# Query transposes of six batches moved from PE to DVE, with loads by groups of 32 features

## Chip, cores and metric

One core of one Trainium2 chip. The metric is the device time of one execution in microseconds. Short names: PE is the matmul engine, DVE the vector engine, ACT the scalar engine, POOL is GpSimd, SP the engine whose queue issues nearly all transfers. The granted clock is the clock that PE was allowed, as a share of its full speed; the mean of a run was 0.976 to 0.993 in the runs told here.

## The reference

```python
# q, k, v: (8 batches, 8 heads, 576 rows, 64 features), fp32
kv  = np.einsum('bhsd,bhse->bhde', k, v)
out = np.einsum('bhsd,bhde->bhse', q, kv)
rms = np.sqrt(np.mean(out * out, axis=-1, keepdims=True) + 1e-06)
x   = (out / rms * g_norm)              # reordered to (4608 tokens, 512)
h   = x @ w_in                          # 512 -> 2048
y   = np.maximum(h, 0.0) ** 2 @ w_out   # 2048 -> 512
```

## The kernel before

It works in nine strips of 512 tokens. Each strip has an "up" part (x @ w_in, relu squared) and a "down" part (@ w_out). In strips 1 to 8 both are made of seven products by a Strassen scheme, and in strip 0 the down part alone is. Between the products it puts the attention of later strips in slices. The product with kv takes a query with its features on the partitions, so each pair of heads is transposed there, against the identity, and copied out of PSUM by ACT:

```python
    def load(b, p, q_eng):              # a pair of heads: k, v, q
        ...
        whole = src[b, hs, 0 : C * P].rearrange("h (sp c) d -> sp h c d", c=C)
        ...                             # q and k, one transfer a head, pieces of 256 bytes
        t = qkv_pool.tile([P, C, 2, D], FP32, name=n, tag=n)
        for h in range(2):
            eng.dma_start(out=t[:, :, h, :], in_=whole[:, h])

    def transposed_query(b, p):
        t = main.pop(("q", b, p))
        ps = apsum.tile([P, C, P], FP32, name="t_ps", tag="at")
        for c in range(C):              # C = 4
            nc.tensor.transpose(ps[:, c, :], flat(t[:, c]), ident)
        qT[b, p] = qt_pool.tile([P, C, P], FP32, name="qT", tag="qT")
        nc.scalar.copy(qT[b, p], ps)
        if b % 2:                       # the last 64 rows of two batches, as one tile
            ...                         # one more transpose (tr_ps) and copy (qT_rest)

    def out_rows(n):                    # which rows of the output a tile of 128 tokens is
        ...
        return [(slice(0, P), out[b * S : b * S + C * P, :].rearrange("(sp c) e -> c sp e", c=C)[c_b])]

    def stream():                       # the next block of w_out, 1 MB, three buffers
        ...
            nc.sync.dma_start(out=w_blk[u], in_=w_out[B_OUT[u[1]]])

    def down(s, p, i):                  # product p of the down part, half i
        ...
        product(p, i, lambda fc: a[:, fc, ts(i, P)], lambda fc: w[:, fc, :], FQ)
        if i == 0: return
        ...
        stream()                        # asks for a block when a product is done
        ...                             # store: copy to o_sb, then SP issues out_rows
```

Products of one part run in the order 1, 2, 6, 5, 7, 3, 4. Each has one of the PSUM banks A (two buffers), B and C.

Of the kernel before, what the change touches and what calls it, by code (L numbers as in the profile page):

```python
# [9 lines left out]
FP32 = mybir.dt.float32  # L10
# [9 lines left out]
def kernel(  # L20
# [26 lines left out]



    nc = tc.nc  # L50
    P = 128
    B, H, S, D = q.shape
# [3 lines left out]
    NP = H // 2  # L56
    FC = d_ff // P
    C = S // P
# [5 lines left out]
    STRIP = NT * P  # L64
    TH = STRIP // 2
    N_STRIP = N_TILE // NT
    EPS = 1e-6
    const = ctx.enter_context(tc.tile_pool(name="const", bufs=1))
    wpool = ctx.enter_context(tc.tile_pool(name="wpool", bufs=1))
    qkv_pool = ctx.enter_context(tc.tile_pool(name="qkv", bufs=3))  # L70
    rest_pool = ctx.enter_context(tc.tile_pool(name="rest", bufs=1))
    qt_pool = ctx.enter_context(tc.tile_pool(name="qt", bufs=NP + 1))
# [18 lines left out]
    def load(b, p, q_eng):  # L91
        hs = slice(2 * p, 2 * p + 2)
        for n, src, eng in (("k", k, nc.sync), ("v", v, nc.sync), ("q", q, q_eng)):
            whole = src[b, hs, 0 : C * P].rearrange("h (sp c) d -> sp h c d", c=C)
            if n == "v":
                t = qkv_pool.tile([P, 2, C, D], FP32, name=n, tag=n)
                eng.dma_start(out=t, in_=whole)  # L97
            else:
# [4 lines that stand above are left out]
            main[n, b, p] = t  # L103
# [4 lines left out]
    v_rest = const.tile([P, 2, H, D], FP32, name="v_rest")  # L108
    q_rest = {}

    def load_rest(b, eng):
        h = b % 2
        half = slice(REST * h, REST * (h + 1))
        if h == 0:
            q_rest[b // 2] = rest_pool.tile([P, H, D], FP32, name="q_rest", tag="q_rest")
        for t, src in ((k_rest[half], k), (v_rest[half, h], v), (q_rest[b // 2][half], q)):
            eng.dma_start(out=t, in_=src[b, :, C * P : S].rearrange("h s d -> s h d"))

    units = [(b, p) for b in range(B) for p in range(NP)]
    to_load = iter(units)  # L120
# [1 line left out]
    def load_next(q_eng=nc.sync):  # L122
        u = next(to_load, None)
        if u is not None:
            load(*u, q_eng)
# [105 lines left out]
    def convert(n):  # L231
        while converted[0] < min(n, len(conversions)):
            fn, a = conversions[converted[0]]
            fn(a)
            converted[0] += 1

    nc.gpsimd.memset(k_rest, 0.0)
    nc.gpsimd.memset(v_rest, 0.0)
    load_next(nc.gpsimd)
    load_rest(0, nc.gpsimd)  # L240
    for i in range(2):
        load_next(nc.gpsimd)
# [12 lines left out]
    qT, kvd, x_n, xt = {}, {}, {}, {}  # L255
    flat = lambda t: t.rearrange("p h d -> p (h d)")

    def transposed_query(b, p):
        t = main.pop(("q", b, p))
        ps = apsum.tile([P, C, P], FP32, name="t_ps", tag="at")  # L260
        for c in range(C):
            nc.tensor.transpose(ps[:, c, :], flat(t[:, c]), ident)  # L262
        qT[b, p] = qt_pool.tile([P, C, P], FP32, name="qT", tag="qT")
        nc.scalar.copy(qT[b, p], ps)
        if b % 2:
            t = q_rest[b // 2][:, 2 * p : 2 * p + 2]
            ps = apsum.tile([P, P], FP32, name="tr_ps", tag="at")
            nc.tensor.transpose(ps, flat(t), ident)
            qT["rest", b // 2, p] = qt_pool.tile([P, P], FP32, name="qT_rest", tag="qT_rest")
            nc.scalar.copy(qT["rest", b // 2, p], ps)  # L270

    def key_value(b, p):
        tk, tv = main.pop(("k", b, p)), main.pop(("v", b, p))
        ps = apsum.tile([P, P], FP32, name="kv_ps", tag="at")
        for c in range(C):
            nc.tensor.matmul(ps, lhsT=flat(tk[:, c]), rhs=tv[:, :, c, :], start=(c == 0), stop=False)  # L276
        nc.tensor.matmul(  # L277
            ps, lhsT=flat(k_rest[:, 2 * p : 2 * p + 2]), rhs=v_rest[:, b % 2, 2 * p : 2 * p + 2],
            start=False, stop=True,
        )  # L280

        d = kv_pool.tile([P, P], FP32, name="kvd", tag="kvd")
        nc.gpsimd.memset(d[0:D, D:P], 0.0)
        nc.gpsimd.memset(d[D:P, 0:D], 0.0)
        nc.scalar.copy(d[0:D, 0:D], ps[0:D, 0:D])
        nc.scalar.copy(d[D:P, D:P], ps[D:P, D:P])
        kvd[b, p] = d
        if b < 2:
            if p == 0:
                load_next(nc.sync if b else nc.gpsimd)  # L290
        else:
            load_next()
            if p == NP - 1 and b + 1 < B:
                load_rest(b + 1, nc.sync)

    def query(n):
# [17 lines left out]
        nc.vector.reduce_sum(out=ms, in_=by_head(sq), axis=AX.X)  # L314
        nc.vector.tensor_scalar(out=ms, in0=ms, scalar1=1.0 / D, scalar2=EPS, op0=ALU.mult, op1=ALU.add)
        r = small.tile([P, H], FP32, name="rms", tag="rms")
# [35 lines left out]
    for b in range(B):  # L352
        for p in range(NP):
            slices += [(transposed_query, (b, p)), (key_value, (b, p))]
        first = b // 2 * PAIR + (C if b % 2 else 0)
        ns = list(range(first, first + C + b % 2))
        for i, n in enumerate(ns + [None]):
            if n is not None:
                slices.append((query, (n,)))
            if i > 0:  # L360
                slices.append((features, (ns[i - 1],)))
                if ns[i - 1] % NT == NT - 1:
                    if ns[i - 1] // NT:
                        slices.append((sums_x, (ns[i - 1] // NT,)))
                    ready[ns[i - 1] // NT] = len(slices)
    slice_at = [0]

    def attend(n):
        while slice_at[0] < min(n, len(slices)):
            fn, a = slices[slice_at[0]]  # L370
            fn(*a)
            slice_at[0] += 1

    def out_rows(n):
        m, c = divmod(n, PAIR)
        if c == C:
            return [
                (slice(REST * h, REST * (h + 1)), out[(2 * m + h) * S + C * P : (2 * m + h + 1) * S, :])
                for h in range(2)
            ]  # L380
        b, c_b = (2 * m, c) if c < C else (2 * m + 1, c - C - 1)
        return [(slice(0, P), out[b * S : b * S + C * P, :].rearrange("(sp c) e -> c sp e", c=C)[c_b])]

    ORDER = (1, 2, 6, 5, 7, 3, 4)
    BANK = {1: "A", 6: "A", 7: "A", 4: "A", 5: "B", 3: "B", 2: "C"}
# [85 lines left out]
    w_blk[0, 1], w_blk[0, 2], w_blk[0, 5] = w_first  # L471
    to_stream = iter([(s, p) for s in range(N_STRIP) for p in ORDER if (s, p) not in w_blk])

# [6 lines left out]
    def down(s, p, i):  # L480
        if i == 0:
            open_bank(p)
        a = gq[s, {1: 11, 2: 21, 6: 11, 5: 1, 7: 12, 3: 21, 4: 22}[p]]
        w = w_blk[s, p]
        product(p, i, lambda fc: a[:, fc, ts(i, P)], lambda fc: w[:, fc, :], FQ)
        if i == 0:
            return
        del w_blk[s, p]
        if s > 0 or p not in (1, 2, 5):
            stream()  # L490
        if p == 1:
            minus(nc.vector, gq[s, 11], gq[s, 1], gq[s, 11])
        if p == 2:
            minus(nc.vector, gq[s, 21], gq[s, 21], gq[s, 11])

        def store(th, eh):
            def f(b, a=None):
                o = osb_pool.tile([P, 2, DH], FP32, name="o_sb", tag="o_sb")
                if a is None:
                    nc.scalar.copy(o, b)  # L500
                else:
                    nc.vector.tensor_tensor(out=o, in0=b, in1=a, op=ALU.add)
                for t in range(2):
                    for part, rows in out_rows(NT * s + 2 * th + t):
                        nc.sync.dma_start(out=rows[:, ts(eh, DH)], in_=o[part, t, :])
            return f

        combine(p, store(0, 0), store(0, 1), store(1, 0), store(1, 1))

    for i in range(ready[0]):  # L510
        attend(i + 1)
        convert((i + 1) // 4)
    for s in range(N_STRIP):
        attend(ready[s])
# [76 lines left out]
```

## Time and profile before

| | |
|---|---|
| median of the first three runs | 1031.32 us |
| PE, DVE, ACT busy | 96 %, 41 %, 26 % of the span |
| PE's waits, all of the span | 33.6 us, nearly all before 175 us |
| transposes of queries on PE | 144, in slots of 0.109 us |

The profile comes from one execution. In a row of the timeline, the first column is the start in microseconds from the beginning of the span and the second is how long the merged row lasted; `x4` is the number of instructions, and `[20.13 <-PE ps_A L399]` is how long the engine was idle before and what released it. In a list of waits the numbers are the total wait, how often, and the longest. Line numbers differ between the kernels: L399 of before is L442 of the changed kernel. The lines that carry the bound are shown in the prediction.

### The profile page before, as it was taken

Reading aid. Unit: us, or ns where it says so; the run is one execution under the profiler, and the core shown is the slowest. Engines: PE = TensorE matmul, PEld = TensorE weight load, DVE = VectorE, ACT = ScalarE, POOL = GpSimd, SP = SyncE. Lnnn points to the kernel's source line nnn. Section 1 sums busy time; section 2 is a strip of 40 time slices with the busy share of each in tenths; the row PEclk is TensorE's granted clock in tenths of the full one; section 3 lists DMA queues with packets and bytes.
Section 4 is the critical chain, followed back from the end, with each engine's and each line's share of the span. In section 5 each row is a group of like instructions: output and inputs, shape, how many; then the busy total and the mean of one; then the engine's idle time right before and its main releaser. Section 6 shows DMA issues by size and latency. Waiting matters only on the chain.

```text
span 1029.7 us, 12226 instructions
## 1 busy us (share of the span) xinstructions
PE 992.0 (96%) x4864; PEld 852.2 (83%) x4864; DVE 423.9 (41%) x769; ACT 264.0 (26%) x546; POOL 19.5 (2%) x83
## 2 busy tenths in 40 slices
PE   3599999999999999999999999999999999999998
PEld 3444688888888888888888888888888888888887
DVE  2777974344233533333333325332632334413420
ACT  3568620321033112221132113210321122102200
POOL 4000000000000000000000000000000000000000
PEclk9699999999999999999999999999999999999999
DMA  9389797134422433244413640274012420251032
GB/s 222 121 235 276 240 326 226 47 81 135 156 82 62 138 133 102 62 114 145 145 32 85 187 163 1 62 207 165 33 31 95 159 74 1 92 175 61 1 133 71
DMA packets 119081, 125.58 MB, mean 122 GB/s; under 512 B 78224, under 2 KB 102800, under 8 KB 111344
## 3 DMA queue, kind: packets, MB, share of 16 engines
q1 hardware_dynamic: 118336, 123.36, 39.2%
q0 software_dynamic: 528, 1.44, 0.6%
q8 instruction: 38, 0.62, 0.2%
q14 instruction: 19, 0.16, 0.0%
q10 hardware_dynamic: 160, 0.00, 0.0%
HBM read 108.00 MB, written 16.78 MB: 121 GB/s over the span
## 4 chain that ended last, share of the span: by engine, by line
PE 87%; DVE 4%; DMA 4%; ACT 3%; SPq 1%; issue 1%; DVEq 0%; ACTq 0%
PE ps_A L399 45%; PE ps_B L399 23%; PE ps_C L399 11%; PE x_ps L309 3%; DMA raw<-in_moe_w_in_dram 2%; PE kv_ps L276 2%; PE xt_ps L336 2%; DMA raw<-in_moe_w_out_dram 2%; PE t_ps L262 1%; ACT w_c L161 1%; DVE wt L195 1%; SPq L97 1%; ACT raw L164 1%; DVE w_c L185 1%; PE kv_ps L277 1%
## 5 line engine op out<-in xcount | busy, mean ns | idle before, releaser
L399 PE MATMUL ps_A<-w_blk,gt 128*128 128x256 f32 x1120 | 249.9, 379 | 0.0
L399 PEld LDWEIGHTS ps_A<-w_blk,gt 128*128 128x128 f32 x1120 | 211.1, 190 | 27.9 <-PE x_ps L304 0.2
L399 PE MATMUL ps_A<-x_t,w_in 128*128 128x256 f32 x768 | 181.6, 379 | 0.6 <-DVE gt L459 0.6
L399 PEld LDWEIGHTS ps_A<-x_t,w_in 128*128 128x128 f32 x768 | 143.8, 190 | 19.5 <-DVE gt L459 1.0
L399 PE MATMUL ps_B<-w_blk,gt 128*128 128x256 f32 x544 | 121.5, 379 | 0.0
L399 PEld LDWEIGHTS ps_B<-w_blk,gt 128*128 128x128 f32 x544 | 102.4, 190 | 13.6 <-issue 0.2
L195 DVE TENSOR_TENSOR gt<-gt 128x512 f32<-128x512 f32 (+1 forms) x54 | 66.2, 1225 | 68.2 <-PE ps_A L399 37.6
L409 ACT COPY snap<-ps_A 128x512 f32<-128x512 f32 x82 | 48.1, 586 | 164.8 <-PE ps_A L399 164.8
L459 DVE TENSOR_TENSOR gt<-ps_C,snap 128x512 f32<-128x512 f32 x32 | 22.1, 692 | 147.8 <-PE ps_C L399 147.8
L460 DVE SCALAR_TENSOR_TENSOR gt<-gt 128x512 f32<-128x512 f32 x96 | 66.4, 692 | 3.3
L459 DVE TENSOR_TENSOR gt<-ps_A,snap 128x512 f32<-128x512 f32 x32 | 22.1, 691 | 108.4 <-PE ps_A L399 108.1
L399 PE MATMUL ps_B<-x_t,w_in 128*128 128x256 f32 x256 | 60.5, 379 | 0.0
L399 PE MATMUL ps_B<-xT,w_in 128*128 128x256 f32 x256 | 60.5, 379 | 0.0
L399 PE MATMUL ps_A<-xT,w_in 128*128 128x256 f32 x256 | 60.5, 379 | 0.0
L399 PE MATMUL ps_C<-xT,w_in 128*128 128x256 f32 x256 | 60.5, 379 | 0.0
L399 PE MATMUL ps_C<-w_blk,gt 128*128 128x256 f32 x256 | 57.7, 380 | 0.0
L314 DVE TENSOR_REDUCE ms<-sq 128x8 f32<-128x512 f32 x36 | 24.6, 684 | 76.9 <-ACT sq L312 76.9
L399 PEld LDWEIGHTS ps_C<-xT,w_in 128*128 128x128 f32 x256 | 48.6, 190 | 6.6
L399 PEld LDWEIGHTS ps_A<-xT,w_in 128*128 128x128 f32 x256 | 48.2, 190 | 6.3
L399 PEld LDWEIGHTS ps_C<-w_blk,gt 128*128 128x128 f32 x256 | 47.7, 190 | 6.2 <-issue 0.2
L399 PEld LDWEIGHTS ps_B<-x_t,w_in 128*128 128x128 f32 x256 | 47.6, 190 | 5.9
L399 PEld LDWEIGHTS ps_B<-xT,w_in 128*128 128x128 f32 x256 | 47.6, 190 | 5.9
(83 smaller groups left out, 867.7 us busy)
## 6 DMA issues: line engine op xcount, KB each, us to landing
w_blk<-w_out SPq DMA_DIRECT2D x60, 1024.0 KB, 5.2
k<-in_k_dram SPq DMA_DIRECT2D x64, 128.0 KB, 3.3
v<-in_v_dram SPq DMA_DIRECT2D x32, 256.0 KB, 3.6
raw<-in_moe_w_in_dram SPq DMA_DIRECT2D x16, 512.0 KB, 5.1
raw<-in_moe_w_out_dram SPq DMA_DIRECT2D x16, 512.0 KB, 5.4
out_dram<-o_sb SPq DMA_DIRECT2D x64, 128.0 KB, 5.0
q<-in_q_dram SPq DMA_DIRECT2D x56, 128.0 KB, 3.4
w_out<-wt SPq DMA_DIRECT2D x8, 512.0 KB, 4.5
```

What stands on the lines that cost most here:

```text
L97: eng.dma_start(out=t, in_=whole)
L161: nc.scalar.activation(c, high_f, AF.Abs)
L164: nc.scalar.activation(r, low, AF.Copy, scale=2.0**-29)
L195: eng.tensor_tensor(out=out, in0=a, in1=b, op=ALU.subtract)
L276: nc.tensor.matmul(ps, lhsT=flat(tk[:, c]), rhs=tv[:, :, c, :], start=(c == 0), stop=False)
L309: nc.tensor.matmul(o, lhsT=qT[b, p][:, c_b, :], rhs=kvd[b, p], start=True, stop=True)
L314: nc.vector.reduce_sum(out=ms, in_=by_head(sq), axis=AX.X)
L336: nc.tensor.transpose(ps[:, p, :], t[:, ts(p, P)], ident)
L399: nc.tensor.matmul(bank[BANK[p]][:, i, :], lhsT=lhsT(k), rhs=rhs(k), start=p in (1, 5, 2) and i == 0 and k == 0, stop=k == n - 1, skip_gro ...
L409: nc.scalar.copy(snap[p], b)
L459: nc.vector.tensor_tensor(out=o, in0=b, in1=a, op=ALU.add)
L460: nc.vector.scalar_tensor_tensor(out=o, in0=o, scalar=0.0, in1=o, op0=ALU.max, op1=ALU.mult)
```

## The change

The intent is to relieve PE, the bound. The change transposes on DVE in squares of 32x32 (SQ = 32): the load puts each group of 32 features of a pair of heads on its own 32 partitions, with 16 rows of 32 features behind one another on each; one DVE instruction (STREAM_TRANSPOSE, 128x512) then gives features on partitions and tokens along the row. Its price is that a load has pieces of 128 bytes and comes in four transfers, and that the tokens come in a permuted order, which the stores undo in four pieces of 32 rows. Batches 0 and 1 stay on PE.

```diff
+    SQ = 32
+    Q_ON_PE = 2
...
+            if n == "q" and b >= Q_ON_PE:
+                t = qkv_pool.tile([P, 4 * C, SQ], FP32, name=n, tag=n)
+                for a in range(4):
+                    h, f = divmod(a * SQ, D)
+                    eng.dma_start(
+                        out=t[ts(a, SQ)],
+                        in_=src[b, 2 * p + h, 0 : C * P, f : f + SQ].rearrange("(i k) f -> i k f", k=4 * C),
+                    )
...                                      (load_rest: 8 small transfers in place of one)
     def transposed_query(b, p):
         t = main.pop(("q", b, p))
+        if b >= Q_ON_PE:
+            qT[b, p] = qt_pool.tile([P, C, P], FP32, name="qT", tag="qT")
+            nc.vector.transpose(out=flat(qT[b, p]), in_=flat(t))
+            if b % 2 and p == NP - 1:
+                rest = qt_pool.tile([P, NP, 4, SQ], FP32, name="qT_rest", tag="qT_rest4", bufs=1)
+                nc.vector.transpose(
+                    out=rest, in_=squares(q_rest[b // 2]).rearrange("p k q f -> p q k f")
+                )
...
+            return
...
-        return [(slice(0, P), out[...].rearrange("(sp c) e -> c sp e", c=C)[c_b])]
...                                      (batches 0 and 1 as before)
+        return [
+            (ts(k, SQ), rows.rearrange("(i k) e -> k i e", k=4 * C)[4 * c_b + k]) for k in range(4)
+        ]
```

More of the change, by code (lines that the diff above doesn't have):

```diff
@@ L94, in load @@
             whole = src[b, hs, 0 : C * P].rearrange("h (sp c) d -> sp h c d", c=C)
-            if n == "v":
+            if n == "q" and b >= Q_ON_PE:
[6 more added lines that the diff above has]
+                    )
+            elif n == "v":
                 t = qkv_pool.tile([P, 2, C, D], FP32, name=n, tag=n)
@@ L109 @@
     q_rest = {}
+    squares = lambda t: t.rearrange("p h d -> p (h d)").rearrange("p (k q f) -> p k q f", k=4, f=SQ)
     def load_rest(b, eng):
@@ L116, in load_rest @@
         for t, src in ((k_rest[half], k), (v_rest[half, h], v), (q_rest[b // 2][half], q)):
-            eng.dma_start(out=t, in_=src[b, :, C * P : S].rearrange("h s d -> s h d"))
+            if src is q and b >= Q_ON_PE:
+                t = squares(q_rest[b // 2])
+                for a in range(4):
+                    hq, f = divmod(a * SQ, D)
+                    for kq in range(2):
+                        eng.dma_start(
+                            out=t[ts(a, SQ), 2 * h + kq],
+                            in_=src[b, hq::2, C * P + kq * SQ : C * P + (kq + 1) * SQ, f : f + SQ].rearrange(
+                                "p i f -> i p f"
+                            ),
+                        )
+            else:
+                eng.dma_start(out=t, in_=src[b, :, C * P : S].rearrange("h s d -> s h d"))
     units = [(b, p) for b in range(B) for p in range(NP)]
@@ L259, in transposed_query @@
         t = main.pop(("q", b, p))
+        if b >= Q_ON_PE:
[5 more added lines that the diff above has]
+                    out=rest, in_=squares(q_rest[b // 2]).rearrange("p k q f -> p q k f")
+                )
+                for i in range(NP):
+                    qT["rest", b // 2, i] = rest[:, i].rearrange("p k f -> p (k f)")
+            return
         ps = apsum.tile([P, C, P], FP32, name="t_ps", tag="at")
@@ L381, in out_rows @@
         b, c_b = (2 * m, c) if c < C else (2 * m + 1, c - C - 1)
-        return [(slice(0, P), out[b * S : b * S + C * P, :].rearrange("(sp c) e -> c sp e", c=C)[c_b])]
+        rows = out[b * S : b * S + C * P, :]
+        if b < Q_ON_PE:
+            return [(slice(0, P), rows.rearrange("(sp c) e -> c sp e", c=C)[c_b])]
+        return [
+            (ts(k, SQ), rows.rearrange("(i k) e -> k i e", k=4 * C)[4 * c_b + k]) for k in range(4)
+        ]
     ORDER = (1, 2, 6, 5, 7, 3, 4)
```

## The prediction

> **What bounds the kernel now.** I read first the shares of each engine and the forty slices, then the waits of PE, then the order of PE's work in one strip, and last the end of the program. The page and its chain of waits:
>
> ```profile
> PE 992.0 (96%) x4864; PEld 852.2 (83%) x4864; DVE 423.9 (41%) x769; ACT 264.0 (26%) x546; POOL 19.5 (2%) x83
> ...
> PE   3599999999999999999999999999999999999998
> ...
> PEclk9699999999999999999999999999999999999999
> DMA  9389797134422433244413640274012420251032
> ...
> PE 87%; DVE 4%; DMA 4%; ACT 3%; SPq 1%; issue 1%; DVEq 0%; ACTq 0%
> ```
>
> PE is the bound: 96% busy, and from the third slice on every slice is at 9 or more. DVE (41%) and ACT (26%) have much room, and so have the DMA engines after the first 200 us. The chain that ended last is PE for 87% of the span. A busy PE alone is weak evidence, so I looked for its waits. This is the list of what PE waited for, whole:
>
> ```profile
> PE xt_ps L336 <- DVE x_n L325: 11.5, 4, 5.9
> PE t_ps L262 <- POOL ident masks.py:199: 9.4, 1, 9.4
> PE tr_ps L268 <- ACT qT L264: 3.7, 2, 2.2
> PE t_ps L262 <- DMA q<-in_q_dram: 3.4, 1, 3.4
> PE kv_ps L276 <- ACT qT L264: 2.9, 1, 2.9
> PE kv_ps L276 <- DMA v<-in_v_dram: 1.3, 1, 1.3
> PE ps_A L433 <- ACT xT L337: 0.8, 1, 0.8
> PE ps_A L399 <- DVE gt L459: 0.6, 1, 0.6
> ```
>
> (Columns: who waited for whom, us in all, times, longest.) Together 33.6 us, and the busy time by stretches puts nearly all of it into the first 200 us (PE is busy 69.6 of the first 100, 97.4 of the second, and 100 of 100 in each from 200 to 820). The query transposes of batches 0 and 1, which wait here, stay on PE. The six batches that the change moves run in the part where PE waits for nothing. So an instruction taken off PE there shortens the span by the slot it held, and by no more. That slot is read from the timeline of PE around two of the groups to be removed:
>
> ```profile
> 545.33 0.60 PE L262 MATMUL t_ps<-ident,q 128*128 128x128 f32 x4
> 545.76 0.27 PE L268 MATMUL tr_ps<-ident,q_rest 128*128 128x128 f32 x1
> 545.87 1.89 PE L399 MATMUL ps_A<-x_t,w_in 128*128 128x256 f32 x8
> ...
> 553.90 1.89 PE L399 MATMUL ps_A<-x_t,w_in 128*128 128x256 f32 x8
> 555.62 0.60 PE L262 MATMUL t_ps<-ident,q 128*128 128x128 f32 x4
> ```
>
> The first column is the start, the second the duration. Matmuls overlap: the durations (273 ns for one transpose) are no cost. The cost is from start to start: 545.76 - 545.33 = 0.43 us for four transposes, 545.87 - 545.76 = 0.11 us for the fifth, about 0.109 us each.
>
> [...]
>
> **The change part by part.**
>
> Off PE: 6 batches x 4 pairs x 4 = 96 transposes of whole tiles, and 3 x 4 = 12 of the rests, in all 108 of 144. 108 x 0.109 = **11.8 us off the path**. The order of everything else on PE stays, as the comparison of instruction orders shows.
>
> Off ACT: 24 copies of 586 ns and 12 of 273 ns, 17.3 us. ACT isn't the bound: worth 0.
>
> Onto DVE: 24 transposes into qT and 3 for the rests, each 128x512, [...]. PE waits for DVE where a bank is to be freed: product 4 needs bank A after DVE has read product 7, with one product (1.73 us) between. The order of DVE in the changed kernel has each transpose behind a product's own two operations, never between the product and the read that frees its bank. [...] Worth 0, at worst some tenths a group.
>
> Query loads: two transfers a pair of heads become four, of 128-byte pieces instead of 256. 24 x 1024 = 24,576 packets more, and 3,072 more for the rests (8 transfers of 128 pieces in place of 512 pieces, per batch), on top of 119,081. A load of k, v and q (2,304 packets) took about 3.3 us of all 16 engines around 541 us (sum of the DMA shares of those slices), 23 ns a packet on one engine; so 27,648 packets are some 40 us of the 16 engines' time (estimate), spread over 500 us where they are a third busy. The loads are issued three pairs ahead, some 30 us before use, and the k, v and q of a pair land in 3.3 to 3.6 us. Hidden.
>
> DMA queue of SP: each issue holds it. 24 x 2 more query issues at 0.59 us (28 us), 6 x 7 more for the rests at 0.63 (26 us), and the permuted token order splits each of the 48 half-width output stores of batches 2 to 7 in four: 144 more at about 0.39 (56 us). These 110 us fall where SP now waits: its list of waits has 282.5 us for ps_A and 256.2 us for kv_ps alone. The danger is a late w_out block behind these issues. A block is asked for when a product ends and needed two products later, 2 x 6.91 = 13.8 us; it lands in 5.2 us (10.1 at worst). A store of eight pieces in front of it takes 8 x 0.39 = 3.1 us, a query and rest load in front some 4 to 6 us more than now. Normally that fits; with the worst landing it does not quite.
>
> The end: here the stores are on the path.
>
> ```profile
> 1023.77 1.89 PE L399 MATMUL ps_A<-w_blk,gt 128*128 128x256 f32 x8
> 1023.99 1.27 PEld L399 LDWEIGHTS ps_A<-w_blk,gt 128*128 128x128 f32 x6
> 1025.70 0.59 ACT L500 COPY o_sb<-ps_A 128x512 f32<-128x512 f32 x1 [20.13 <-PE ps_A L399]
> 1026.31 0.81 SPq L505 DMA_DIRECT2D out_dram<-o_sb  x2
> ```
>
> After the last matmul comes one copy, then two issues in 0.81 us, then 2 us to landing. The last strip is of batch 7, so two become eight, one behind the other: 6 x 0.39 = **2.3 us onto the path**; a smaller piece may land a little sooner, so I take 2.2.
>
> Sum: 1031.3 - 11.8 + 2.2 = **1021.7 us**, 0.9% less.
>
> **The rivals.**
> (1) The whole gain and more, past 2%: that needs 20.6 us. 108 transposes at 190 ns would give it, but the starts show 109 ns; and there are no waits of PE behind 200 us to be freed. I see no way to it.
> (2) DVE becomes the wait: it blocks in order on a query transfer or on its own queue, and PE waits for a bank. For it: one wait of PE on DVE of 0.6 us shows that the margin is thin at one place. Against: DVE idles over half of each strip, waiting for products of PE. If each of 27 transposes cost PE 0.3 us, 8 us come back: 1030 us.
> (3) A late block of w_out behind the many issues on SP. For it: the arithmetic above, with some 3 us to spare in bad cases. Against: three buffers, and landings of 5.2 us mostly. Two us in each of the five or six strips with loads: 1032 us.
> (4) Stores cost more than at the end alone, if a 32-row store is issued or lands slower than I take it: another 1 to 3 us at the end.
>
> **Range and chances.** The 11.8 us are firm to within 0.5 and the 2.2 to within 1. The rivals 2 and 3 can only add time, so the range is longer above: 1019.5 to 1026.0, predicted 1021.8. Faster by over 2% (below 1010.7) 0.02; slower by over 2% (above 1051.9) needs a failure of the DMA schedule in every strip, 0.02; within 2% 0.96.
>
> **What would show it right or wrong.** PE has 4864 - 108 = 4756 matmuls, and is still at 100 of 100 us in the stretches from 200 to 820; its list of waits has no new row above 1 us. [...] The time from the last matmul to the end grows by about 2.2 us, with eight issues near 0.39 us in it. The w_blk transfers still land in about 5 us. If PE shows waits for DVE products of L459 or idles in the first down products of a strip, rival 2 or 3 holds. [...]

## The result

The changed kernel took **1022.45 us** (median of four runs, 1021.19 to 1022.73), against 1031.09 us for the kernel before (four runs). The ratio is 0.9915, with a 95 % interval of 0.9897 to 0.9932. A ratio is the mean time of one kernel's runs over that of the other's in the same rounds, so it isn't quite the ratio of the medians. The gain is under 2 %, but the interval leaves 1 well outside.

The page of the changed kernel, its busy row, the slices of PE and the chain:

```profile
PE 979.3 (96%) x4756; PEld 842.2 (83%) x4756; DVE 440.2 (43%) x796; ACT 248.6 (24%) x510; POOL 19.6 (2%) x83
...
PE   3599899999999999999999999999999999999997
...
PE 87%; DMA 4%; DVE 4%; ACT 3%; SPq 1%; issue 1%; DVEq 0%; ACTq 0%
```

108 instructions are gone from PE, and PE is the bound as before. What PE waited for, those rows that begin to matter:

```profile
PE xt_ps L373 <- DVE x_n L362: 14.7, 4, 5.9
...
PE ps_A L442 <- DVE gt L502: 0.6, 1, 0.6
```

There is no new row. After 190 us the last one alone remains, as before. At the place that the prediction showed, the transposes are gone from the timeline of PE:

```profile
537.39 1.89 PE L442 MATMUL ps_C<-xT,w_in 128*128 128x256 f32 x8
539.11 1.89 PE L442 MATMUL ps_A<-x_t,w_in 128*128 128x256 f32 x8
```

539.11 - 537.39 = 1.72 us is the slot of the product alone; in the kernel before 0.43 and 0.11 us of transposes stood between these two. DVE's timeline shows where the work went:

```profile
540.11 0.69 DVE L503 SCALAR_TENSOR_TENSOR gt<-gt 128x512 f32<-128x512 f32 x1
540.72 0.70 DVE L288 STREAM_TRANSPOSE qT<-q 128x512 f32<-128x512 f32 x1
544.56 0.69 DVE L502 TENSOR_TENSOR gt<-ps_A,snap 128x512 f32<-128x512 f32 x1 [3.14 <-PE ps_A L442]
```

Behind the transpose DVE still waits 3.14 us for PE. The end of the program, first the copy, then the row of the last stores from the view of the tile o_sb (durations of one issue: least, median, most; first and last start):

```profile
1014.45 0.59 ACT L543 COPY o_sb<-ps_A 128x512 f32<-128x512 f32 x1 [20.13 <-PE ps_A L442]
```
```profile
L548 SPq DMA_DIRECT2D out_dram<-o_sb x8: 314/419/421, 1015.1 to 1018.2; - x8
```

To account for the 9.0 us between the two profiled spans (1029.7 and 1020.7), I cut each at two marks: the first matmul of strip 1, and ACT's copy behind the last matmul.

| profiled run | to strip 1 | strip 1 to last copy | last copy to end | span |
|---|---|---|---|---|
| before | 175.00 | 850.70 | 4.0 | 1029.7 |
| changed | 175.60 | 838.85 | 6.25 | 1020.7 |
| difference | +0.6 | -11.85 | +2.25 | -9.0 |

The middle stretch turned out to be a very sharp measure: over the runs below it repeats to 0.01 us when nothing in it changes. The first stretch is not: it lies between 173.1 and 175.6 us in ten of the twelve profiles, with no order by kernel, so the 0.6 is noise. Another run of the changed kernel had 173.1.

### The profile page after: what moved, and what is told of

The parts are those of the page before. It is cut to its first block, busy times and chain, and to the rows that moved or that the text cites. A ratio compares the mean times of both kernels' runs of the same rounds, so it can differ in the third digit from the quotient of the medians.

```text
span 1020.7 us, 12318 instructions
## 1 busy us (share of the span) xinstructions
PE 979.3 (96%) x4756; PEld 842.2 (83%) x4756; DVE 440.2 (43%) x796; ACT 248.6 (24%) x510; POOL 19.6 (2%) x83
## 3 DMA queue, kind: packets, MB, share of 16 engines
q1 hardware_dynamic: 149728, 123.38, 40.9%
## 4 chain that ended last, share of the span: by engine, by line
PE 87%; DMA 4%; DVE 4%; ACT 3%; SPq 1%; issue 1%; DVEq 0%; ACTq 0%
PE ps_A L442 45%; PE ps_B L442 23%; PE ps_C L442 12%; PE x_ps L346 3%; DMA raw<-in_moe_w_out_dram 2%; PE kv_ps L313 2%; DMA raw<-in_moe_w_in_dram 2%; PE xt_ps L373 2%; ACT w_c L187 1%; DVE w_c L211 1%; SPq L109 1%; DVE wt L221 1%; ACT raw L190 1%; PE kv_ps L314 1%; SPq L114 0%
```

## The experiments

The theory: the gain is the slots on PE and the loss the longer end; nothing else that the change adds reaches the path. Rivals: the gain came from freed copies or PSUM buffers; DVE's work holds PE up somewhere; or the many issues on SP do. All kernels gave correct results. This table has them all, in the order told below; "median" and "ratio" are of the timed runs, the three stretches of the profiled one.

| run | to strip 1 | strip 1 to copy | to end | median us | ratio to before |
|---|---|---|---|---|---|
| e0 changed kernel again | 173.1 | 838.84 | 6.2 | 1021.20 | 0.9900 |
| e2 PE transposes put back, unread | 173.3 | 850.70 | 6.25 | 1034.16 | 1.0018 |
| e4 before, stores split only | 175.4 | 850.70 | 6.4 | 1034.03 | 1.0020 |
| e1 rows in order, stores whole | 174.7 | 838.85 | 3.7 | 1019.58 | 0.9885 |
| e3 each DVE transpose three times | 173.7 | 838.85 | 6.2 | 1021.55 | 0.9908 |
| e3b each nine times | 175.1 | 880.37 | 6.25 | 1063.84 | 1.0316 |
| e6 loads by 16 features | 177.2 | 853.91 | 6.2 | 1033.78 | 1.0032 |
| e8 loads by 8 rows | 174.1 | 841.08 | 6.2 | 1023.98 | 0.9942 |
| e7 = e1 with loads by 16 | 174.2 | 843.87 | 3.7 | 1023.84 | 0.9936 |
| e5 = e1 with all batches on DVE | 189.4 | 838.84 | 3.8 | 1034.03 | 1.0025 |

**e0: the changed kernel again.** No edit.

> The changed kernel unaltered, for noise and as the measure of the other runs of this call. Mine: 1022.3 us within 1.5; from the start of strip 1 on PE to the last copy 838.9 us within 0.3 (before: 850.7); from the last copy to the end 6.2 us within 0.3 (before: 4.0). If the 0.6 us by which strip 1 began later than before in the first profile belong to the change, they come again; if they are noise of the start, they do not.

838.84 and 6.2 us came again, and the 0.6 us of a later start did not.

**e2: the transposes of PE put back.** Their results go to PSUM and nobody reads them.

```diff
             nc.vector.transpose(out=flat(qT[b, p]), in_=flat(t))
+            ps = apsum.tile([P, C, P], FP32, name="t_ps", tag="at")
+            for c in range(C):
+                nc.tensor.transpose(ps[:, c, :], flat(t)[:, ts(c, P)], ident)
+            if b % 2: ...                # the same for the rest, tr_ps
```

> The changed kernel with the 108 transposes of PE put back where they were, their results unread. Theory (a removed transpose is worth its slot of 0.109 us on PE and nothing else in the change has a cost inside the strips): 11.8 us more than the changed kernel, about 1034 us, 2.3 us above the kernel before, and 850.7 us from strip 1 to the last copy. Rival (the gain came from the copies taken off ACT or the PSUM buffers set free, or PE hides such transposes): clearly less than 11 us comes back.

The stretch is 850.70 us again, to the hundredth that of the kernel before, although ACT makes none of the moved copies and DVE makes the transposes of the six batches as well. So the gain is the slots: 11.85 / 108 = 0.110 us each. The copies taken off ACT were worth nothing. The PSUM buffers came back together with the transposes, so this run alone does not part the two; but 0.110 us is the slot read from the starts, and in the kernel before PE has after 190 us no wait for such a buffer, only the 0.6 us for bank A.

**e4: the stores alone.** The kernel before, whose stores of batches 2 to 7 are cut in four.

```diff
-        return [(slice(0, P), out[b * S : b * S + C * P, :].rearrange("(sp c) e -> c sp e", c=C)[c_b])]
+        rows = out[b * S : b * S + C * P, :].rearrange("(sp c) e -> c sp e", c=C)[c_b]
+        if b < 2:
+            return [(slice(0, P), rows)]
+        return [(ts(k, 32), rows[ts(k, 32)]) for k in range(4)]
```

> The kernel before with only its stores of batches 2 to 7 split in four pieces of 32 rows, nothing else. Theory: slower by the longer end alone, 2.25 us, about 1033.3 us, with 850.7 us from strip 1 to the last copy and 6.2 us after it. Rival (the issues on SP hold back blocks of weights): PE shows waits inside the strips and the loss is over 4 us.

The stretch keeps its 850.70 us and the end has 6.4: 2.4 us more than before, and the median is 2.5 us above that of the kernel before in the same call (1031.56). As the stores stand, they cost at the end alone.

**e1: rows in order.** The token order is not forced: partition i may take rows i, 32+i, 64+i and so on. Then the squares come out in the order of the rows, and an output tile is 128 rows in order.

```diff
-   in_=src[b, 2 * p + h, 0 : C * P, f : f + SQ].rearrange("(i k) f -> i k f", k=4 * C),
+   in_=src[b, 2 * p + h, 0 : C * P, f : f + SQ].rearrange("(k i) f -> i k f", k=4 * C),
...
-        return [ (ts(k, SQ), rows.rearrange("(i k) e -> k i e", k=4 * C)[4 * c_b + k]) for k in range(4) ]
+        return [(slice(0, P), rows[ts(c_b, P)])]
```

> The changed kernel with partition i of a 32-feature load taking rows i, 32+i, 64+i ... instead of 16i to 16i+15, so that an output tile is 128 rows in order and its store is one transfer again; the loads keep their number and their piece of 128 bytes. Theory (four-fold stores cost only at the end): the end is 4.0 us instead of 6.25, the span 2.25 us less than the changed kernel, about 1020.0 us; the stretch from strip 1 to the last copy stays 838.9. Rival (the split stores or their 144 issues also cost inside the strips): the stretch itself shrinks, and the gain is more than 3 us. Rival (the new row order makes the loads slow): the queries land later than 3.0 us.

The end is 3.7 us and the stretch 838.85: the 2.5 us at the end are won back and nothing is lost. The medians differ by 1.6 us only, and the intervals of the two ratios overlap (0.9881 to 0.9918 and 0.9868 to 0.9901), so it is the end that shows the gain, not the medians. This version has the lowest median of all, 1019.58 us, 1.15 % below the kernel before.

**e3 and e3b: more work on DVE.** Each transpose is made three times, or nine, into the same tile.

```diff
-            nc.vector.transpose(out=flat(qT[b, p]), in_=flat(t))
+            for _ in range(3):           # 9 in e3b; the rests likewise
+                nc.vector.transpose(out=flat(qT[b, p]), in_=flat(t))
```

> The changed kernel with each of its 27 transposes on DVE made three times, 37 us more work on DVE at the places where the change put it. Theory (DVE's added work lies in its idle time): 838.85 us from strip 1 to the last copy as in the changed kernel, at most 1 us more, and no new row in what PE waits for. Rival (a DVE instruction between products holds back a bank and part of it reaches PE): 54 extra instructions times some 0.3 us, 15 us and more.

> Each of the 27 transposes on DVE made nine times, 6.3 us in a row at each place and 150 us in all. DVE would still be busy under 60 % of the span. If only DVE's share mattered, nothing would change. Mine: 6.3 us is more than the 3 to 4 us for which DVE waits behind a transpose now (3.14 us in front of the next read of bank A around 541 us), so product 4 waits for bank A and the span grows by 1 to 3 us at most of the 24 places, 30 to 70 us in all, with a new row of PE waiting for L502.

Three times changed nothing at all: 838.85 us with DVE at 478.5 us busy instead of 440.2. Nine times cost 41.5 us with DVE at 56 % of the span, inside what I expected. PE's waits after 190 us in e3b:

```profile
PE ps_A L444 <- DVE gt L504: 26.5, 13, 7.3
PE x_ps L343 <- DVE qT_rest L293: 3.6, 2, 3.2
```

It is the wait that I expected (bank A, read by DVE), at 12 of the 24 places; the thirteenth wait is the old one of 0.6 us. The waits of these two rows grew by 29.5 us, and 9.8 of the other 12.0 us are slower matmuls behind the five longest waits for bank A (3.4 us four times, 7.3 us once); these five places cost 5.1 to 9.8 us each. At the first of them the eight matmuls behind the wait held 332.77 - 329.47 = 3.30 us, where eight hold 1.73 us elsewhere. The seven waits of 0.7 us cost 1.0 us each; I had expected 1 to 3 us a place. So it is not DVE's share of the span that foretells the loss, but the length of the piece of work between two products: 2.1 us in a row fit everywhere, 6.3 us at half of the places.

**e6: shorter pieces and more of them.** Each load of 32 features is made by two of 16.

```diff
+                    for e in range(2):
+                        eng.dma_start(
+                            out=t[ts(a, SQ), :, ts(e, SQ // 2)],
+                            in_=src[..., f + e * 16 : f + e * 16 + 16].rearrange("(i k) f -> i k f", k=4 * C),
+                        )
```

> The changed kernel with each query load of 32 features made by two loads of 16: pieces of 64 bytes instead of 128, eight transfers a pair of heads instead of four, 49,152 packets and 96 issues more. Theory (the loads are hidden): 838.85 us from strip 1 to the last copy within 0.3, span as the changed kernel. Rival (short pieces hold up k, v or the weights): new waits of PE for a DMA, or for DVE standing at a transpose, some us in each of the six strips with loads.

Here my theory missed: it was some 12 us slower than the changed kernel. Two places account for the 15.06 us by which the stretch grew in the profiled run (which was the slowest of the four): start for start against the changed kernel, PE fell behind by 9.04 us at the first and by 6.03 us at the second. The first, at the start of strip 1, from ACT's timeline:

```profile
185.78 0.58 ACT L546 COPY o_sb<-ps_A 128x512 f32<-128x512 f32 x1 [28.56 <-DMA out_dram<-o_sb]
186.27 0.59 ACT L455 COPY snap<-ps_A 128x512 f32<-128x512 f32 x1
```

ACT waits for an output buffer whose store SP could issue only behind the loads of batch 2, and the copy behind it (snap), which PE needs, is late: PE waits 6.1 us there. The second, from PE's timeline, and the windows around it (PE busy and count, granted clock, DMA share, GB/s):

```profile
708.44 10.16 PE L445 MATMUL ps_B<-w_blk,gt 128*128 128x256 f32 x32 [2.78 <-DMA w_blk<-w_out]
```
```profile
704.00:705.50 1.50, 1.50 (x8) 1.00 0.65 208
705.50:708.40 2.90, 0.15 (x1) 0.88 1.01 407
708.40:711.00 2.60, 2.56 (x6) 0.50 1.02 410
711.00:714.00 3.00, 3.00 (x8) 0.50 0.71 262
```

A block of w_out came 2.78 us late, and the 32 matmuls took 10.16 us in place of 7.07, because the granted clock was 0.50 for some 6 us behind the gap. A wait of 2.8 us cost 6.0, and at the first place one of 6.1 us cost 9.0: there eight matmuls behind it took 3.78 us in place of 1.89. This is the rival of a late block, which the prediction named and which the change itself had not shown. How near it had come is in SP's timelines. Of the changed kernel:

```profile
674.00 4.13 SPq L548 DMA_DIRECT2D out_dram<-o_sb  x8
...
684.61 3.95 SPq L136 DMA_DIRECT2D q_rest<-in_q_dram  x8
688.66 6.75 SPq L521 DMA_DIRECT2D w_blk<-w_out  x3
```

The product that frees the buffer ended at 679.01, but SP came to the block only at 688.66, and the product that needs it (bank B) began at 694.89: 6.2 us from request to use. In the kernel before it was 703.95 - 689.75 = 14.2 us. In the changed kernel's own trace this block landed 4.7 us after its request (the view of the tile w_blk, window 688.6:689), so it was 1.5 us early; in e0 it was 1.0 us early. No other block of the strips had so little. In e6 it took 5.5 us. Rows in order has more, since its stores take 0.84 us of SP where the changed kernel's take 4.13, and its four query loads 2.06 where those take 2.62:

```profile
684.26 10.27 SPq L519 DMA_DIRECT2D w_blk<-w_out  x3
```

There the use is at 694.01, 9.75 us later, and the block lands in 5.0.

**e8 and e7: issues, or short pieces?** e8 cuts each load by rows instead, so there are as many issues as in e6, but with pieces of 128 bytes. e7 puts the loads of 16 features on the rows-in-order kernel.

```diff
+                    whole_a = src[...].rearrange("(i k) f -> i k f", k=4 * C)   # e8
+                    for e in range(2):
+                        eng.dma_start(
+                            out=t[ts(a, SQ), 2 * C * e : 2 * C * (e + 1)],
+                            in_=whole_a[:, 2 * C * e : 2 * C * (e + 1)],
+                        )
```

> The changed kernel with each query load cut in two by rows, not by features: eight transfers a pair of heads as in the run with 16 features, but pieces of 128 bytes and as many packets as the changed kernel. If the number of issues on SP is what made that run slow, this one is slow too: about 1033 us, with PE waiting for a w_out block by 1 to 3 us around 700 us and a late start of strip 1. If the short pieces did it, this one is as the changed kernel, 1021 to 1022 us.

> The loads of 16 features again, but on the rows-in-order kernel, whose stores are one transfer each. In the strip where the block for the product into bank B came 2.8 us late, SP had spent 5.4 us on eight pieces of a store; two stores take about 0.9. If the late block comes from the queue of issues on SP, it is asked for some 4.5 us earlier and is in time: no wait of PE for a DMA behind 190 us, 838.85 us from strip 1 to the last copy. If it comes from 64-byte pieces loading the DMA engines, the wait stays.

e8 came out between: 1.5 to 3 us slower than the changed kernel, not 12. Its stretch is 2.2 us longer, from one wait of 1.9 us at the start of strip 1 (the same one, for ACT's copy); the block at 690.54 was in time by a hair: it landed in 4.9 us, 0.2 us before its use. So more issues alone do harm there, but the larger part of e6's loss needs the 64-byte pieces, twice as many in all, as well. They hold SP longer: eight loads took 5.29 us in e6 and 3.92 us in e8. The traces show that this queue on SP, more than the landing, made the block late: from the free buffer to the request passed 13.2 us in e6 (689.61 to 702.81) and 10.8 in e8 (679.75 to 690.54), from request to landing 5.5 and 4.9. And among these query loads it is the number of pieces in an issue, not their length, that went with its time on SP. By the shortest group of loads in SP's timeline after 640 us, one took 2.61 / 4 = 0.65 us with 512 pieces of 128 bytes (changed kernel), 5.29 / 8 = 0.66 with 512 of 64 (e6), and 3.86 / 8 = 0.48 with 256 of 128 (e8). The row order went with it as well: with rows in order it was 0.52 us for 512 pieces of either length (2.06 / 4 in e1, 4.13 / 8 in e7). e7 had no late block, as expected, and a 3.1 us wait at the start of strip 1 was still there, so the stretch was not the 838.85 us that I expected. I had overlooked it: the stores there are of batches 0 and 1 and were never split. Of 5.0 us lost, 3.1 are that wait, and most of the rest is slower work behind it: eight matmuls took 3.09 us in place of 1.89, and four transposes 1.06 in place of 0.60.

**e5: all batches on DVE.** Q_ON_PE = 0 on the rows-in-order kernel.

> The rows-in-order kernel with the queries of batches 0 and 1 on DVE as well, no query transpose left on PE. 36 more slots of 0.109 us are 3.9 us of PE, but in the first 200 us PE waits for weights and conversions on DVE and ACT anyhow, DVE is full there (100 to 120 us: all of the time), and GpSimd has to issue more loads at the start. Mine: no gain, between 1 us less and 4 us more than 1019.6. If the slots counted as they do later: 1015.7. If it is slower, strip 1 begins later than 175 us and PE waits for k, v or q at the start.

From strip 1 on nothing changed (838.84), but strip 1 began 14.6 us later than in e1. The largest waits of PE:

```profile
PE kv_ps L313 <- DMA v<-in_v_dram: 14.3, 3, 7.1
PE xt_ps L373 <- DVE x_n L362: 13.9, 3, 7.1
PE x_ps L341 <- DVE qT_rest L291: 7.4, 1, 7.4
```

So in the first part PE waits above all for transfers and DVE, and leaving batches 0 and 1 on PE was right. Which of the changes at the start (more loads, or transposes on a full DVE) costs most, this run does not separate. I expected a loss of at most 4 us; it was 14.5.

## Why the prediction was right

- **The slots.** Foretold 11.8 us off PE, from starts 0.43 and 0.11 us apart, since PE waited for nothing there. The stretch shortened by 11.85 us, and e2 gave back exactly that. The duration of 273 ns would have foretold 29 us.
- **The end.** Foretold 2.2 us; 2.25 measured (from spans rounded to 0.1 us), 2.4 in e4, and undone by e1. The issues follow each other at (1018.2 - 1015.1) / 7 = 0.44 us, slower than the 0.39 taken, and the small last store lands in 1.6 us, sooner than 2.0. That these two small misses cancel is luck.
- **DVE.** No trace before the result had a transpose on DVE, so its time was not shown beforehand. In the changed kernel 24 transposes of 0.704 us and 3 of 0.667 make 18.9 us. (DVE's busy time, which counts overlapping instructions once, rose by 16.3.) Worth 0, which e3 shows for three times the work.
- **ACT.** From 264.0 to 248.6 us busy (15.4 us less, where 17.3 were foretold), worth 0, as e2 shows.
- **Loads.** The count of packets grew by 31,392, not 27,648. The difference, 3,744, is 16 for each of the 48 + 42 + 144 = 234 further issues. Their time was overrated: the hardware queue's share went from 39.2 % of 1029.7 to 40.9 % of 1020.7 us, 14 us in place of 40.
- **SP.** The direction was right, the margin was thinner than told. The block was some 8 us later than before, as worked out (3.1 for the store, 4 to 6 for the loads), but in the strips eight stores took 3.6 to 5.1 us, not 3.1, and the "some 3 us to spare" were 1.5 us at the tightest place, 1.0 in e0. The prediction's own terms didn't give 3 us either: 13.8 - 5.2 - 3.1 - 4 to 6 leaves 1.5 at best. This third rival did not come true in the profiled runs of the change, but e6 and e8 show that it stood at the door.
- **Slips without effect.** "From the third slice on every slice is at 9 or more" isn't so for the last one, which is at 8: that is the end of the program. The sum gives 1021.7 us, the range names 1021.8.

## What to carry to other kernels

Price an instruction on a full engine by the distance between starts, not by its duration (here 0.110 us, not 0.273), and then look for what the change adds where nothing hides it, above all at the end of the program. When work moves to an engine or a queue with idle time, its share of the span says little (DVE at 56 % of it cost 41.5 us in e3b): what counts is how long a piece stands in front of something the bound engine needs, and how much of the slack it leaves for the next change. If a layout permutes rows, look for the order that keeps the stores whole.

## Figures to keep from these runs

- A transpose of 128x128 in fp32 on PE has a record of 273 ns, but in a stream of other matmuls it was worth 0.110 us (11.85 us for 108).
- Each gap in PE's work that was followed up cost more than its own length: one of 2.78 us (e6) had the granted clock at 0.50 for some 6 us behind it and cost 6.0, one of 3.1 us (e7) cost 5.0, one of 1.9 us (e8) cost 2.2. So in these runs the length of the gap alone doesn't foretell the loss.
- SP needed 0.34 us to issue a block of 1 MB, about 0.42 for 32 rows of 1 KB at the end, and 0.65 for a load of 512 pieces of 128 bytes, which landed in 3.0 us; a queue of such issues made a block wait 9.6 us (688.66 - 679.01).
- An fp32 transpose on DVE took 0.704 us for 128x512, and 0.667 us with a rearranged input; a tensor_tensor of the same size took 0.691 us.
